# Chunk 0 of a fused attention and MLP kernel: score units on two bank pairs, another order of loads, and idle TensorE time filled for longer

## The chip, the cores and the metric

One core of a Trainium2 chip. The metric is device time in microseconds (us) of one execution. Three runs of the kernel before took 676.94, 677.34 and 677.88 us; their median is 677.34.

## The reference

Attention with 4 sink keys and a window of 128, then an MLP whose activation is a leaky ReLU with a slope per hidden unit. All inputs are fp32; q, k and v are 4 x 8 x 768 x 64 (batch, heads, sequence, head size), the MLP is 512 to 2048 to 512 on 3072 tokens.

```python
scores = scale * np.matmul(q, k.transpose(0, 1, 3, 2))
keep = is_sink | in_window          # pos_k < 4, or 0 <= pos_q - pos_k < 128
scores = np.where(keep, scores, -1000000000.0)
scores = scores - np.max(scores, axis=-1, keepdims=True)
a = np.exp(scores)
a = a / (np.sum(a, axis=-1, keepdims=True) + 1e-09)
...
x = np.ascontiguousarray(attn_out.transpose(0, 2, 1, 3)).reshape(B * S, H * D)
h = x @ w_in
g = np.maximum(h, 0.0) + alpha * np.minimum(h, 0.0)
return (g @ w_out).astype(np.float32)
```

## The kernel before, in words

**Chunks.** The 3072 tokens are 12 chunks of 256 (three per batch entry). For each chunk the attention of 8 heads gives x, transposed, in a high and a low part (xh, xl); then come 16 blocks f of 128 hidden units. gemm1(c, f) makes h from three products per slice of x (high x high, low x high, high x low: L894), ACT and DVE make g and split it into gh and gl (L898 to L901), and gemm2(c, f) adds g times the second weight block to two PSUM banks (L929 to L932). Weights arrive as float64, 1 MB per block, and are split into a high and a low fp32r part on the chip: ACT takes the magnitude (L382), DVE shifts and merges bits (L386, L387, L396; for f from 8 on L394), then the high part is cast (L401; ACT by default, DVE where the planner finds that earlier) and DVE subtracts for the low part (L404). gemm1(c, f) waits for the whole split block f.

**Attention of chunks 0 and 1 (SPLIT).** Two heads share a tile with their q and k in rows 0 to 63 and 64 to 127, `pairs` in DRAM. A score unit is (pair of heads, half u of the queries): two matmuls of 64 rows each into two PSUM banks (L588), then per head DVE's masked minimum (L610, which reads the bank) and ACT's exp (L614). For u = 0 of chunk 0 a unit has 132 columns instead of 260, since there are no earlier keys. After both halves PE transposes the softmax (L633, L634), ACT or DVE copies it out (`comb`, L638, L639), POOL copies the sink columns (L625); after four heads follow the sink tiles `ts` (L689, L690, transposed at L708, read out at L711 as `sinkT`), the reciprocal sums (`ob`, L679, L820), the products with v (L786), and xh and xl (L837, L841, L845). gemm1(0, 0) reads the first xl.

**PSUM.** Eight banks in four kinds of two: `s` for scores (banks 0, 1), `pa` for transposes and products (2, 3), `h` for gemm1 (4, 5), `o` for gemm2 (6, 7; chunk 0's attention borrows them for transposes). In the rows of the instruction order below the banks are numbered from 64, so `s` is 64 and 65, `pa` 66 and 67, `h` 68 and 69, `o` 70 and 71. pt_87 to pt_89 are the three softmax tiles, wa_95 and wa_96 the two work tiles of the weight split, w_305 the first split weight block.

**What sets the order.** All work is written down as operations with a cost, and a planner (`draw`) simulates the five engines, picking by time and rank and giving out tiles as they come free; `issue` then emits the instructions in that order, so each engine runs a fixed queue, in order. Chunk 0's attention goes first; `work` spreads the later chunks' attention over the gemm steps: chunk 1's over OVER = 4 of the first LEAD = 7 steps. Loads of the start are issued by SP in the order in which the program lists them: parameters, three head pairs, weight block 0, the rows `vs` for the sinks, the fourth pair, v, weight blocks 1 to 3, chunk 1's pairs.

**Fillers.** While the plan's time is below WARM = 28 us, `issue` fills a gap before a PE operation with idle matmuls (L1086, 128x512, bf16), each counted as 0.22 us (0.44 in the first 5 us). They all write bank 5, the second `h` bank. 35 of them are in the program.

Of the kernel before, what the change touches and what calls it, by code (L numbers as in the profile page):

```python
# [19 lines left out]
P = 128  # L20
B, H, S, D = 4, 8, 768, 64
DM, DF = 512, 2048
NS = 4
WIN = 2 * P + NS
QC = 2 * P
KC = 3 * P + 2 * NS
# [7 lines left out]
WAIT = {"DVE": 0.2, "ACT": 0.2, "PE": 0.1}  # L34
FILL = 0.22
COLD = 5.0
WARM = 28.0
PENALTY = 0.3
LATEST = 12
BIG = 1e30  # L40
# [2 lines left out]
SPLIT = (0, 1)  # L43
PAIRED = 3
LEAD = 7
OVER = 4
LATE = 14
SPAN = 12
AHEAD = 4
# [29 lines left out]
class Plan:  # L79
# [6 lines left out]
    def __init__(self, tc):  # L86
        self.tc, self.nc = tc, tc.nc
        self.free, self.turn = {}, {}
        self.ops, self.rank, self.last = [], 0, {}

    def kind(self, name, tiles):
        self.free[name] = [(0.0, t) for t in tiles]
# [60 lines left out]
    def draw(self, start, shift=None, until=None):  # L153
# [17 lines left out]
        clock = dict.fromkeys(self.ENGINES, start)  # L171
# [3 lines left out]
        while len(steps) < len(ops):  # L175
# [43 lines left out]
            o, e, t = best[3:]  # L219
            for x in o.ways:  # L220
                open_[x].remove(o)
            got = []
            for v in o.takes:
                if v not in at:
# [34 lines left out]
    def issue(self, steps, fill=None, until=0.0):  # L259
        for o, e, t, clock, got in steps:  # L260
            for v, tile_ in got:
                v.at = tile_
            if e == "PE" and fill and t < until:
                step = FILL * (2 if t < COLD else 1)
                while t - clock > step + 0.2:
                    self.emit(fill)
                    clock += step
            self.emit(o.ways[e][1])

# [52 lines left out]
def program(ctx, tc, qk, pairs, vp, vq, vs, w, par, out):  # L322
# [109 lines left out]
    def bound(v):  # L432
        if v.at is None:
            v.at = v.bind()
        return v.at

    def load_head(c, h):
        if c in SPLIT and h % 2:
            stage[c, h] = stage[c, h - 1]
            return  # L440
        t = stage[c, h] = val("stage") if c else early[h // 2]
        src = pairs[c, h // 2] if c in SPLIT else qk[c, h]
        op("SP", ISSUE, lambda: nc.sync.dma_start(bound(t), src), writes=[t], nbytes=4 * P * (QC + KC))

    def load_v(c, p):
        if c == 0:
            two = early_v[p:p + 2]
            vtile[c, p], vtile[c, p + 1] = two

            def run():  # L450
                for t in two:
                    bound(t)
                nc.sync.dma_start(two[0].box["tile"][:, p:p + 2].rearrange("p n a h d -> p n (a h d)"),
                                  vp[c, p:p + 2].rearrange("n p x -> p n x"))
            op("SP", ISSUE, run, writes=two, nbytes=8 * P * 6 * D)
            return
        t = vtile[c, p] = val("v")
        op("SP", ISSUE, lambda: nc.sync.dma_start(t.at.rearrange("p a h d -> p (a h d)"), (vq if c >= PAIRED else vp)[c, p]),
           writes=[t], nbytes=4 * P * 6 * D)
# [21 lines left out]
    def then(run):  # L481
        n = len(plan.ops)
        run()
        for o in plan.ops[n:]:
            if o.nbytes or o is plan.ops[n]:
                o.rank = len(plan.ops) - 1000
    then(lambda: setup("SP", ISSUE, lambda: nc.sync.dma_start(param, par), (), ("param",)))
    then(lambda: load_head(0, 0))
    then(lambda: load_head(0, 2))
    then(lambda: load_head(0, 4))  # L490
    then(lambda: load_weights(0, "SP"))
    then(lambda: vs_prep(0))
    then(lambda: load_head(0, 6))
    then(lambda: load_v(0, 0))
    then(lambda: load_v(0, 2))
    for f in range(1, FIRST):
        then(lambda: load_weights(f, "SP"))
# [54 lines left out]
    def prep_head(c, h):  # L552
        st = stage.pop((c, h))
        if c in SPLIT:
            r = slice(h % 2 * D, (h % 2 + 1) * D)
            prep[c, h] = (st, r)
            return
        kq = val("kq")
        ks, qh, ql = [lambda s=s: kq.at[:, s] for s in (slice(0, KC), slice(KC, KC + QC), slice(KC + QC, KC + 2 * QC))]
        q_raw, k_raw = lambda: st.at[:, :QC], lambda: st.at[:, QC:]  # L560
        op("ACT", cast(KC), lambda: nc.scalar.copy(ks(), k_raw()), reads=[st], writes=[(kq, "k")])  # L561
        op("ACT", cast(QC), lambda: nc.scalar.copy(qh(), q_raw()), reads=[st], writes=[(kq, "q")])
        op("DVE", dve(KC), lambda: nc.vector.tensor_tensor(ks()[D:], k_raw()[D:], ks()[D:].bitcast(F32), ALU.subtract),  # L563
           reads=[st], writes=[(kq, "k")])
        op("DVE", dve(QC), lambda: nc.vector.tensor_tensor(ql(), q_raw(), qh().bitcast(F32), ALU.subtract),
           reads=[st, (kq, "q")], writes=[(kq, "l")])
        prep[c, h] = (kq, qh, ql, ks)

    def unit(c, h, u):
        if h == 0 and u == 0:  # L570
            nms[c], sink[c], sums[c] = val("nm"), val("sink"), val("sm")
            if c in SPLIT:
                s0 = sink[c]
                op("POOL", 0.15, lambda: nc.gpsimd.memset(s0.at, 0.0), writes=[s0])
        ko = u * (P + NS)
        qs = slice(u * P, (u + 1) * P)
        w0 = slice(0 if c % CPB or u else P, WIN)
        n = w0.stop - w0.start
        kw = slice(ko + w0.start, ko + WIN)
        if c in SPLIT:  # L580
            pair = (h, h + 1)
            banks_ = [val("s") for _ in pair]
            used = [prep[c, h][0]]

            def scores():
                for x, bk in zip(pair, banks_):
                    st, r = prep[c, x]
                    nc.tensor.matmul(bk.at[:, w0], st.at[r, :QC][:, qs], st.at[r, QC:][:, kw], start=True, stop=True)  # L588
            op("PE", 1.47 * native(n), scores, reads=used, writes=banks_, tail=N_TAIL, mode="row")
        else:  # L590
            pair = (h,)
            banks_ = [val("s")]
            kq, qh, ql, ks = prep[c, h]

            def scores():
                s = banks_[0].at
                nc.tensor.matmul(s[:, w0], qh()[:, qs], ks()[:, kw], start=True, stop=False)  # L597
                nc.tensor.matmul(s[:, w0], ql()[:, qs], ks()[:, kw], start=False, stop=True)  # L598
            op("PE", 2 * mm(n), scores, reads=[kq], writes=banks_, tail=R_TAIL)
        for x, bk in zip(pair, banks_):  # L600
            soften(c, x, u, bk)
# [480 lines left out]
    idle = const.tile([P, 2], BF16, name="idle")  # L1082
    plan.emit(lambda: nc.vector.memset(idle, 0.0))

    def fill():
        nc.tensor.matmul(banks[5], idle[:, :1].broadcast_to([P, P]), idle[:, 1:].broadcast_to([P, 512]), start=True, stop=True)  # L1086
    plan.link()
    span, steps = plan.draw(0.8)
    plan.issue(steps, fill, WARM)
# [69 lines left out]
def general(nc, gen, ptile, cc, b, qk5, vp5, nsink, window, ident):  # L1159
# [20 lines left out]
    for h in range(H):  # L1180
        q = gen.tile([D, QC], F32, tag="q", name="q")
        k = gen.tile([D, S], F32, tag="k", name="k")
        v = gen.tile([P, S // P, D], F32, tag="v", name="v")
        nc.sync.dma_start(q, qk5[b, cc, h, 0:D, 0:QC])
        for n in range(CPB):
            nc.sync.dma_start(
                k[:, n * QC:(n + 1) * QC].rearrange("p (a x) -> p a x", a=2),
                qk5[b, n, h, 0:D, QC + P:].rearrange("p (a x) -> p a x", a=2)[:, :, NS:])
            nc.sync.dma_start(v[:, 2 * n:2 * n + 2], vp5[b, n, h // 2, :, 1:3, h % 2])
        po = (h % 2) * D  # L1190
        for u in range(2):
# [86 lines left out]
```

## Time and profile before

| | us |
|---|---|
| median of three runs | 677.34 |
| span of the profiled execution | 676.2 |
| PE busy | 663.8 |
| DVE busy | 525.8 |
| ACT busy | 397.5 |
| POOL busy | 34.5 |

The profiled execution is known by its span, from its first to its last instruction; 1.1 us lie between that and the median of the runs, outside the span. PE's busy time includes fillers, and matmuls overlap with their own weight loads (PEld), so a matmul's listed length is longer than the distance to the next one. In timeline rows the columns are start, length, engine, line, operation, tiles, shapes, and in brackets the idle time before it with what ended it. Rows of a table by stretches are explained where they stand.

### The profile page before, as it was taken

Reading aid. Unit: us, or ns where it says so; the run is one execution under the profiler, and the core shown is the slowest. Engines: PE = TensorE matmul, PEld = TensorE weight load, DVE = VectorE, ACT = ScalarE, POOL = GpSimd, SP = SyncE. Lnnn points to the kernel's source line nnn. Section 1 sums busy time; section 2 is a strip of 40 time slices with the busy share of each in tenths; the row PEclk is TensorE's granted clock in tenths of the full one; section 3 lists DMA queues with packets and bytes.
Section 4 is the critical chain, followed back from the end, with each engine's and each line's share of the span. In section 5 each row is a group of like instructions: output and inputs, shape, how many; then the busy total and the mean of one; then the engine's idle time right before and its main releaser. Section 6 shows DMA issues by size and latency. Waiting matters only on the chain.

```text
span 676.2 us, 13243 instructions
## 1 busy us (share of the span) xinstructions
PE 663.8 (98%) x4532; PEld 580.5 (86%) x4534; DVE 525.8 (78%) x1750; ACT 397.5 (59%) x1066; POOL 34.5 (5%) x115
## 2 busy tenths in 40 slices
PE   9989999999999999999999999999999999999996
PEld 4577898888989989989988988988998988998995
DVE  6999999968967976986986995995895994994331
ACT  6989888827636726736636735644744753853332
POOL 2110000001000000000000000010000000000000
PEclk9979999999999999999999999999999999999999
DMA  8684641424343453443443433552542543420001
GB/s 314 229 277 151 241 187 39 127 71 147 122 133 107 122 148 93 145 132 95 141 118 114 143 107 93 163 140 61 172 128 78 161 128 88 142 94 17 32 2 35
DMA packets 58683, 85.19 MB, mean 126 GB/s; under 512 B 9072, under 2 KB 35056, under 8 KB 58608
## 3 DMA queue, kind: packets, MB, share of 16 engines
q1 hardware_dynamic: 55056, 71.17, 34.7%
q10 hardware_dynamic: 3552, 13.11, 5.4%
q8 instruction: 37, 0.61, 0.4%
q14 instruction: 38, 0.31, 0.1%
HBM read 67.22 MB, written 17.04 MB: 125 GB/s over the span
## 4 chain that ended last, share of the span: by engine, by line
PE 83%; DVE 9%; ACT 5%; issue 2%; POOL 0%; DMA 0%; ACTq 0%; SPq 0%; POOLq 0%
PE bank L894 35%; PE bank L931 12%; PE bank L932 11%; PE bank L929 11%; PE bank L786 3%; PE bank L598 3%; PE bank L597 3%; PE bank L875 2%; DVE wa L396 2%; ACT pt L614 1%; ACT wa L382 1%; DVE wa L394 1%; DVE w L404 1%; DVE g L899 1%; DVE gl L901 1%
## 5 line engine op out<-in xcount | busy, mean ns | idle before, releaser
L894 PE MATMUL bank<-xh,w 128*128 128x256 f32 x1536 | 307.9, 283 | 0.4 <-DVE g L899 0.2
L894 PEld LDWEIGHTS bank<-xh,w 128*128 128x128 f32 x1536 | 250.6, 189 | 9.0 <-DVE g L899 3.0
L894 PE MATMUL bank<-xl,w 128*128 128x256 f32 x768 | 215.1, 280 | 0.1
L898 ACT ACTIVATE g<-bank,param 128x256 f32<-128x256 f32 x192 | 90.5, 472 | 117.4 <-PE bank L894 113.1
L931 PE MATMUL bank<-w,gh 128*128 128x512 f32 x382 | 151.7, 397 | 0.2 <-ACT gh L900 0.2
L932 PE MATMUL bank<-w,gh 128*128 128x512 f32 x382 | 150.1, 393 | 0.0
L894 PEld LDWEIGHTS bank<-xl,w 128*128 128x128 f32 x768 | 145.2, 189 | 4.4 <-DVE xl L808 0.3
L614 ACT ACTIVATE pt<-pt,nm 128x260 f32<-128x260 f32 (+1 forms) x192 | 94.5, 493 | 53.5 <-DVE nm L610 53.1
L899 DVE TENSOR_TENSOR g<-bank,g 128x256 f32<-128x256 f32 x192 | 79.7, 419 | 51.4 <-ACT g L898 50.9
L929 PE MATMUL bank<-w,gl 128*128 128x512 f32 x382 | 119.5, 394 | 0.0
L900 ACT CAST gh<-g 128x256 fp32r<-128x256 f32 x192 | 76.9, 404 | 59.7 <-DVE g L899 59.6
L901 DVE TENSOR_TENSOR gl<-g,gh 128x256 fp32r<-128x256 f32 x192 | 80.5, 423 | 26.5 <-ACT gh L900 23.0
L610 DVE CUSTOM_DVE_ANT_0 pt<-bank,masks 128x260 f32<-128x260 f32 (+1 forms) x192 | 75.0, 401 | 19.3 <-PE bank L598 15.5
L929 PEld LDWEIGHTS bank<-w,gl 128*128 128x128 f32 x382 | 70.7, 188 | 16.2 <-issue 0.7
L931 PEld LDWEIGHTS bank<-w,gh 128*128 128x128 f32 x382 | 71.9, 188 | 9.5 <-ACT gh L900 0.7
L932 PEld LDWEIGHTS bank<-w,gh 128*128 128x128 f32 x382 | 71.9, 188 | 8.3
L563 DVE TENSOR_TENSOR kq<-stage,kq 64x392 fp32r<-64x392 f32 x80 | 45.3, 566 | 2.7
L659 POOL TENSOR_TENSOR sink<-pt,ri 128x8 f32<-128x8 f32 x80 | 20.8, 264 | 504.7 <-DVE ri L644 358.8
L597 PE MATMUL bank<-kq 128*128 128x260 f32 (+1 forms) x160 | 44.4, 278 | 1.3 <-DVE nm L610 1.3
L598 PE MATMUL bank<-kq 128*128 128x260 f32 (+1 forms) x160 | 45.0, 281 | 0.0
L655 DVE CUSTOM_DVE_ANT_0 comb<-pt,ri 128x128 f32<-128x128 f32 x136 | 43.1, 343 | 0.4
L561 ACT CAST kq<-stage 128x392 fp32r<-128x392 f32 x80 | 40.9, 512 | 0.7 <-ACT pt L614 0.2
(130 smaller groups left out, 686.9 us busy)
## 6 DMA issues: line engine op xcount, KB each, us to landing
stage<-qk SPq DMA_DIRECT2D x80, 324.0 KB, 2.9
wraw<-w ACTq DMA_DIRECT2D x12, 1024.0 KB, 5.9
swap<-comb SPq DMA_DIRECT2D x36, 256.0 KB, 2.0
comb<-swap SPq DMA_DIRECT2D x36, 256.0 KB, 3.2
v<-vq SPq DMA_DIRECT2D x36, 192.0 KB, 2.5
out_dram<-ob SPq DMA_DIRECT2D x22, 256.0 KB, 3.5
wraw<-w SPq DMA_DIRECT2D x4, 1024.0 KB, 12.0
v<-vp SPq DMA_DIRECT2D x8, 192.0 KB, 6.9
```

The source lines that it names most:

```text
L597: nc.tensor.matmul(s[:, w0], qh()[:, qs], ks()[:, kw], start=True, stop=False)
L598: nc.tensor.matmul(s[:, w0], ql()[:, qs], ks()[:, kw], start=False, stop=True)
L610: op("DVE", dve(n), lambda: nc.vector.tensor_tensor_reduce(out=pt.at[:, u, w0], in0=s.at[:, w0], in1=masks[:, i, w0], scale=-0.125, scalar ...
L614: op("ACT", exp(n), lambda: nc.scalar.activation(pt.at[:, u, w0], pt.at[:, u, w0], AF.Exp, bias=nm.at[:, h, u:u + 1], scale=-1.0, accum_ou ...
L894: nc.tensor.matmul(h(), fin.at[:, 0, part, ks], rhs.at[:, kt], start=(kt == 0 and n == 0), stop=(kt == KT - 1 and n == 2))
L898: op("ACT", act(QC, True), lambda: nc.scalar.activation(g.at, h(), AF.Copy, scale=alt[:, f:f + 1]), reads=[bk, known("param")], writes=[g])
L899: op("DVE", dve(QC), lambda: nc.vector.tensor_tensor(g.at, h(), g.at, ALU.max), reads=[bk], writes=[g])
L900: op("ACT", cast(QC), lambda: nc.scalar.copy(gh.at, g.at), reads=[g], writes=[gh])
L901: op("DVE", dve(QC), lambda: nc.vector.tensor_tensor(gl.at, g.at, gh.at.bitcast(F32), ALU.subtract), reads=[g, gh], writes=[gl])
L929: nc.tensor.matmul(o2[j].at, gl.at[:, js], fin.at[:, 1, 0], start=False, stop=(f == NF - 1))
L931: nc.tensor.matmul(o2[j].at, gh.at[:, js], fin.at[:, 1, 0], start=(f == 0), stop=False)
L932: nc.tensor.matmul(o2[j].at, gh.at[:, js], fin.at[:, 1, 1], start=False, stop=False)
```

## The change

Five things, all at the start of the program:

- Chunk 0's score units take the bank pairs `s` and `h` in turn: u = 0 in `s`, u = 1 in `h` (gemm1 does not use `h` yet).
- SP's order: weight block 0 comes right behind the first head pair, ahead of the other pairs; the first v load comes ahead of the fourth pair.
- q is stored behind k in the tile, so that chunk 0's loads can leave out the 128 keys that it never reads (128x520 instead of 128x648), and the first third of v.
- Fillers are allowed up to WARM = 44 us of the plan, and each goes to a bank that the plan calls vacant at that time, the first found among the kinds `h`, `s`, `pa`, `o`; where there is none, nothing is filled.
- OVER = 5: chunk 1's attention is spread over five steps instead of four.

In the changed kernel the lines after these edits are numbered 2 or 3 higher (L610 is L613, L404 is L406, L1086 is L1089).

```diff
-WARM = 28.0
+WARM = 44.0
-OVER = 4
+OVER = 5
@@ draw
+            if e == "PE":
+                self.vacant[o] = next((f[0][1] for f in map(free.get, ("h", "s", "pa", "o")) if f and f[0][0] <= clock[e]), None)
@@ issue
-            if e == "PE" and fill and t < until:
+            if e == "PE" and fill and t < until and self.vacant[o] is not None:
                 step = FILL * (2 if t < COLD else 1)
                 while t - clock > step + 0.2:
-                    self.emit(fill)
+                    self.emit(lambda: fill(self.vacant[o]))
@@ load_head
+        seen = slice(0 if c else P, KC + QC)
-        op("SP", ISSUE, lambda: nc.sync.dma_start(bound(t), src), writes=[t], nbytes=4 * P * (QC + KC))
+        op("SP", ISSUE, lambda: nc.sync.dma_start(bound(t)[:, seen], src[:, seen]), writes=[t], nbytes=4 * P * (seen.stop - seen.start))
@@ load_v, chunk 0
-                nc.sync.dma_start(two[0].box["tile"][:, p:p + 2].rearrange("p n a h d -> p n (a h d)"),
-                                  vp[c, p:p + 2].rearrange("n p x -> p n x"))
+                nc.sync.dma_start(two[0].box["tile"][:, p:p + 2, 1:].rearrange("p n a h d -> p n (a h d)"),
+                                  vp[c, p:p + 2, :, 2 * D:].rearrange("n p x -> p n x"))
@@ the first loads
     then(lambda: load_head(0, 0))
+    then(lambda: load_weights(0, "SP"))
     then(lambda: load_head(0, 2))
     then(lambda: load_head(0, 4))
-    then(lambda: load_weights(0, "SP"))
     then(lambda: vs_prep(0))
+    then(lambda: load_v(0, 0))
     then(lambda: load_head(0, 6))
-    then(lambda: load_v(0, 0))
     then(lambda: load_v(0, 2))
@@ unit
-            banks_ = [val("s") for _ in pair]
+            banks_ = [val("h" if c == 0 and (h // 2 * 2 + u) % 2 else "s") for _ in pair]
@@ fill
-    def fill():
-        nc.tensor.matmul(banks[5], idle[:, :1].broadcast_to([P, P]), idle[:, 1:].broadcast_to([P, 512]), start=True, stop=True)
+    def fill(bank_):
+        nc.tensor.matmul(bank_, idle[:, :1].broadcast_to([P, P]), idle[:, 1:].broadcast_to([P, 512]), start=True, stop=True)
```

Every `draw` runs again with these numbers, so the order moves on all engines. Two places matter for what follows. The first is DVE's queue in chunk 0, from the second half of the first head pair on; before it stood so (ISA is the masked minimum; the rows that read out its result are left out):

```order
L610 ISA pt_87,nm_99<-bank_64,masks 128x260
L610 ISA pt_88,nm_99<-bank_65,masks 128x260
L610 ISA pt_89,nm_99<-bank_64,masks 128x132
L610 ISA pt_87,nm_99<-bank_65,masks 128x132
L639 COPY comb_91<-bank_70 128x384
L610 ISA pt_89,nm_99<-bank_64,masks 128x260
L610 ISA pt_87,nm_99<-bank_65,masks 128x260
L386 TENSOR_SCALAR wa_95<-wa_95 128x1024
L467 TENSOR_TENSOR vs_112<-ob_113,vs_112 64x512
L674 TENSOR_SCALAR ri_103<-sm_101 128x8
L689 CAST ts_110<-sink_97 128x4x32
```

The same place in the changed kernel:

```order
L613 ISA pt_87,nm_99<-bank_68,masks 128x260
L613 ISA pt_88,nm_99<-bank_69,masks 128x260
L642 COPY comb_91<-bank_70 128x384
L388 TENSOR_SCALAR wa_95<-wa_95 128x1024
L613 ISA pt_89,nm_99<-bank_64,masks 128x132
L613 ISA pt_87,nm_99<-bank_65,masks 128x132
L613 ISA pt_89,nm_99<-bank_68,masks 128x260
L613 ISA pt_87,nm_99<-bank_69,masks 128x260
L389 SCALAR_TENSOR_TENSOR wa_95<-wraw,wa_95 128x1024
L613 ISA pt_88,nm_99<-bank_64,masks 128x132
L677 TENSOR_SCALAR ri_103<-sm_101 128x8
L692 CAST ts_110<-sink_97 128x4x32
```

The comb copy and the first weight step have moved ahead of the second pair's units, the second weight step has moved ahead of the sink tiles, and the `vs` row behind them.

The second place is PE's queue in chunk 1, where the profile shows PE idle before the third pair's units (stage_79 and stage_80 are the tiles of chunk 1's head pairs). Before:

```order
L588 MATMUL bank_64<-stage_80 128x260
L588 MATMUL bank_65<-stage_80 128x260
L633 MATMUL bank_66<-ident,pt_88 128x128
L634 MATMUL bank_66<-ident,pt_88 128x128
L633 MATMUL bank_67<-ident,pt_89 128x128
L634 MATMUL bank_67<-ident,pt_89 128x128
L588 MATMUL bank_64<-stage_79 128x260
L588 MATMUL bank_65<-stage_79 128x260
```

The same place in the changed kernel (the idle matmul stands there four times, each with its weight load):

```order
L591 MATMUL bank_64<-stage_80 128x260
L591 MATMUL bank_65<-stage_80 128x260
L636 MATMUL bank_67<-ident,pt_88 128x128
L637 MATMUL bank_67<-ident,pt_88 128x128
L1089 LDWEIGHTS idle
L1089 MATMUL bank_70<-idle 128x512
L636 MATMUL bank_66<-ident,pt_89 128x128
L637 MATMUL bank_66<-ident,pt_89 128x128
L934 MATMUL bank_70<-w_305,gh_121 128x512
L935 MATMUL bank_70<-w_305,gh_121 128x512
L591 MATMUL bank_64<-stage_79 128x260
L591 MATMUL bank_65<-stage_79 128x260
```

Four fillers and the first half of gemm2(0, 0) have moved in between two score units; that half stood behind chunk 1's first products before. In all there are 30 fillers now, none after these four.

More of the change, by code (lines that the diff above doesn't have):

```diff
@@ L88, in __init__ @@
         self.free, self.turn = {}, {}
-        self.ops, self.rank, self.last = [], 0, {}
+        self.ops, self.rank, self.last, self.vacant = [], 0, {}, {}
     def kind(self, name, tiles):
@@ L452, in run @@
                     bound(t)
-                nc.sync.dma_start(two[0].box["tile"][:, p:p + 2].rearrange("p n a h d -> p n (a h d)"),
-                                  vp[c, p:p + 2].rearrange("n p x -> p n x"))
-            op("SP", ISSUE, run, writes=two, nbytes=8 * P * 6 * D)
+                nc.sync.dma_start(two[0].box["tile"][:, p:p + 2, 1:].rearrange("p n a h d -> p n (a h d)"),
+                                  vp[c, p:p + 2, :, 2 * D:].rearrange("n p x -> p n x"))
+            op("SP", ISSUE, run, writes=two, nbytes=8 * P * 4 * D)
             return
@@ L559, in prep_head @@
         ks, qh, ql = [lambda s=s: kq.at[:, s] for s in (slice(0, KC), slice(KC, KC + QC), slice(KC + QC, KC + 2 * QC))]
-        q_raw, k_raw = lambda: st.at[:, :QC], lambda: st.at[:, QC:]
+        q_raw, k_raw = lambda: st.at[:, KC:], lambda: st.at[:, :KC]
         op("ACT", cast(KC), lambda: nc.scalar.copy(ks(), k_raw()), reads=[st], writes=[(kq, "k")])
@@ L587, in scores @@
                     st, r = prep[c, x]
-                    nc.tensor.matmul(bk.at[:, w0], st.at[r, :QC][:, qs], st.at[r, QC:][:, kw], start=True, stop=True)
+                    nc.tensor.matmul(bk.at[:, w0], st.at[r, KC:][:, qs], st.at[r, kw], start=True, stop=True)
             op("PE", 1.47 * native(n), scores, reads=used, writes=banks_, tail=N_TAIL, mode="row")
@@ L1183, in general @@
         v = gen.tile([P, S // P, D], F32, tag="v", name="v")
-        nc.sync.dma_start(q, qk5[b, cc, h, 0:D, 0:QC])
+        nc.sync.dma_start(q, qk5[b, cc, h, 0:D, KC:])
         for n in range(CPB):
@@ L1187, in general @@
                 k[:, n * QC:(n + 1) * QC].rearrange("p (a x) -> p a x", a=2),
-                qk5[b, n, h, 0:D, QC + P:].rearrange("p (a x) -> p a x", a=2)[:, :, NS:])
+                qk5[b, n, h, 0:D, P:KC].rearrange("p (a x) -> p a x", a=2)[:, :, NS:])
             nc.sync.dma_start(v[:, 2 * n:2 * n + 2], vp5[b, n, h // 2, :, 1:3, h % 2])
@@ L1238 @@
         for half in (slice(0, D), slice(D, P)):
-            qk[:, c, :, half, :QC] = qT[:, c]
-            o = QC
+            qk[:, c, :, half, KC:] = qT[:, c]
+            o = 0
             for n, i in enumerate(blocks):
```

## Prediction

> **What bounds the kernel now.** I read four views: the page, a table by stretches, the chain that ended last in order of time, and the timeline of the first 75 us. First the page's busy times, and the table by stretches (start:end, length, then the busy us of PE, PEld, DVE, ACT and POOL with their instructions, the granted clock, DMA share, GB/s).
>
> ```profile
> PE 663.8 (98%) x4532; PEld 580.5 (86%) x4534; DVE 525.8 (78%) x1750; ACT 397.5 (59%) x1066; POOL 34.5 (5%) x115
> ```
>
> ```profile
> 6.00:14.00 8.00, 7.63 (x44) 3.79 (x43) 4.74 (x21) 6.34 (x21) 1.00 (x4) 1.00 1.00 381
> 14.00:34.00 20.00, 19.10 (x130) 11.88 (x131) 19.37 (x50) 19.12 (x51) 2.91 (x6) 1.00 0.71 257
> 34.00:44.00 10.00, 8.27 (x38) 6.41 (x39) 9.38 (x26) 9.01 (x25) 2.33 (x4) 0.66 0.85 310
> 44.00:70.00 26.00, 25.16 (x181) 20.28 (x182) 24.85 (x42) 21.94 (x47) 0.86 (x2) 1.00 0.57 188
> 70.00:97.00 27.00, 26.97 (x177) 24.35 (x176) 26.63 (x42) 23.55 (x40) 0.00 (x0) 1.00 0.55 200
> 115.00:670.00 555.00, 553.48 (x3839) 495.84 (x3839) 420.15 (x1515) 299.83 (x850) 23.62 (x82) 1.00 0.37 109
> ```
>
> PE's 98% is an average over stages that differ. From 115 to 670 us PE is busy 553.5 of 555 us with matmuls of the reference, and the change leaves those matmuls alone; little is to be won there. Before 44 us PE's busy time holds idle filling and waiting. From 14 us on DVE is the full engine: 19.37 of 20 us, then 9.38 of 10, 24.85 of 26, 26.63 of 27. It has slack only from 6 to 14 us (8 - 4.74 = 3.26 us), from 34 to 44 (0.62) and from 44 to 70 (1.15). So the start is a race of DVE through softmax, weight splitting and the first g tiles, and PE fills up behind it. From 70 us both are full, and there DVE is just in time:
>
> ```profile
> 68.89 1.22 DVE L404 TENSOR_TENSOR w<-wa,w 128x1024 fp32r<-128x1024 f32 x1
> 69.98 0.28 PE L894 MATMUL bank<-xh,w 128*128 128x256 f32 x1
> 74.82 0.19 PEld L894 LDWEIGHTS bank<-xh,w 128*128 128x128 f32 x1 [0.46 <-DVE g L899]
> ```
>
> The eighth weight block is finished by DVE at 70.1 us and its first matmul begins at 70.0, nothing between; at 74.82 PE waits for DVE again. What DVE gains before 70 us therefore comes off the end one for one, provided PE is not behind it. Next the chain in order of time (start, us, what), cut to where PE stands on it:
>
> ```profile
> 5.08 1.60 PE bank L1086 x5
> 6.68 0.64 PE bank L588 x4
> 7.69 1.09 PE bank L1086 x5
> ...
> 38.36 1.58 PE bank L588 x4
> 40.56 2.56 PE bank L894 x12
> ```
>
> Two things are to be seen. Early, the chain runs through idle matmuls (L1086): they stand ahead of a score unit that could not start anyway, because its two banks were still being read. Later it runs through PE at half clock (0.66 on average from 34 to 44 us).
>
> **The change, part by part.**
>
> *Two bank pairs and the second unit at once (chunk 0).* DVE's waits in that stretch:
>
> ```profile
> 7.35 0.43 DVE L610 CUSTOM_DVE_ANT_0 pt<-bank,masks 128x260 f32<-128x260 f32 x1 [1.04 <-PE bank L588]
> 9.23 0.30 DVE L610 CUSTOM_DVE_ANT_0 pt<-bank,masks 128x132 f32<-128x132 f32 x1 [1.10 <-PE bank L588]
> 10.89 0.43 DVE L610 CUSTOM_DVE_ANT_0 pt<-bank,masks 128x260 f32<-128x260 f32 x1 [0.51 <-PE bank L588]
> 12.01 0.69 DVE L386 TENSOR_SCALAR wa<-wa 128x1024 int32<-128x1024 int32 x1 [0.34 <-ACT wa L382]
> 18.33 1.23 DVE L404 TENSOR_TENSOR w<-wa,w 128x1024 fp32r<-128x1024 f32 x1 [0.42 <-ACT w L401]
> 22.26 0.69 DVE L845 TENSOR_TENSOR xl<-ob,xh 128x512 fp32r<-128x512 f32 x1
> ```
>
> They sum to 1.04 + 1.10 + 0.51 + 0.34 + 0.42 = 3.41 us ahead of xl, which opens the first gemm1. With four banks the first pair's four L610 run back to back: the last ended at 7.35 + 2 x 0.43 = 8.2, and without the first wait it ends at 7.1. What is late next is on ACT (and POOL, last row):
>
> ```profile
> 8.33 0.50 ACT L614 ACTIVATE pt<-pt,nm 128x260 f32<-128x260 f32 x1
> 9.61 0.48 ACT L638 COPY comb<-bank 128x384 f32<-128x384 f32 x1 [0.68 <-PE bank L634]
> 10.77 1.12 ACT L382 ACTIVATE wa<-wraw 128x1024 f32<-128x1024 f32 x1
> ...
> 13.05 0.69 POOL L625 COPY sink<-pt 128x8 f32<-128x8 f32 x2 [3.88 <-ACT pt L614]
> ```
>
> The pair's last exp starts at about 7.4 instead of 8.33, so the transposes behind it and DVE's comb copy come at about 8.7 instead of 9.6. In the new order DVE takes that copy and the first weight step ahead of the second pair, and so waits twice: from 7.1 to 8.7 (1.6 us) for the copy, 0.5 long; and from 9.2 to 9.9 (0.7) for ACT, which behind its last exp (8.1) has its own comb copy (0.48) and the first weight step (1.12 and a short read of its sum). The second pair's four L610 then run without a wait. A third wait is new: the sink tiles (L689) now come before the vs row, and follow POOL's two copies (0.69) behind the second pair's exps, another 0.7. The 0.42 before L404 goes: the first block's high part moves from ACT (L401) to DVE, for which the trace has no row; the nearest are L386 (0.69) and L404 (1.23), same 128x1024, and I take 0.69, being a one-input row. Against it one comb copy moves from DVE to ACT, about half a us either way. Sum on DVE: 1.6 + 0.7 + 0.7 = 3.0 for 3.41, and 0.1 because one bad row moves behind the first L610: **0.5 us earlier**, between 0 (each removed wait returns) and 1.0 (the first pair's lead survives).
>
> In the rows of DVE's queue that stand with the change, the copy and the weight step have moved ahead of the second pair: this is where two of the removed waits return.
>
> *First weight block second, unread keys not loaded.* What the loads bring in the first stretches (last column GB/s):
>
> ```profile
> 2.00:4.00 2.00, 2.00 (x6) 0.45 (x3) 1.21 (x9) 0.10 (x1) 0.79 (x5) 1.00 0.86 237
> 4.00:6.00 2.00, 1.91 (x8) 0.91 (x8) 1.90 (x13) 0.00 (x0) 0.54 (x2) 1.00 1.05 286
> 6.00:8.00 2.00, 2.00 (x13) 0.91 (x11) 0.96 (x7) 1.06 (x5) 0.00 (x0) 1.00 0.85 327
> ```
>
> The block now ends 0.01 (parameters) + 0.27 (one shortened pair tile) + 1.05 MB into the queue, 1.33 MB; 237 and 286 GB/s bring 1.05 MB by 6 us and 327 the rest by 6.9. ACT needs it at about 8.7. That cover is 1.8 us; beyond it the price is 1 for 1. The three pair tiles, the vs rows and the v tiles that it passes on SP come later or as before: the second pair tile, behind the block, at about 1.59 MB or 7.7 us, and its scores are not due before 9. SP does nothing here but issue loads. The 0.5 MB not loaded are hidden: apart from the first pair tile no wait on a DMA stands on this stretch of the chain. I put nothing on this part.
>
> *Fill until 44 us.* The half clock and what precedes it (PE rows, then one short stretch):
>
> ```profile
> 31.97 0.39 PE L894 MATMUL bank<-xh,w 128*128 128x256 f32 x2
> 35.69 1.08 PE L588 MATMUL bank<-stage 64*128 64x260 f32 x4 [1.19 <-DVE nm L610]
> 40.78 0.63 PE L894 MATMUL bank<-xh,w 128*128 128x256 f32 x2
> ```
>
> ```profile
> 30.00:32.00 2.00, 1.69 (x12) 1.04 (x12) 2.00 (x5) 1.97 (x6) 0.80 (x2) 1.00 0.79 177
> ```
>
> An idle of 0.31 us in 2 left the clock at 1.00; one of 1.19 was followed by the halving. The Trainium skill (TensorE: Matmul & The Clock Gate, "Why this matters for your kernels") asks only that PE-idle gaps stay under about 3 us. By that rule the 1.19 us gap would have been harmless, the fillers worth nothing, and the sum 676.2 - 0.5 + 1.1 = 676.8; the trace, with the clock at 0.66 behind that gap, disagrees. In the new order, as the rows of PE's queue show, four fillers and the first half of gemm2 of the first weight block stand in that gap. At full clock the chain's pieces shrink: L894 by the ratio 0.63 to 0.39 (2.56 to 1.6), L588 from 1.58 to 0.64: 0.96 + 0.94, PE is some 1.9 us earlier at 44 us. DVE caps what this is worth, since it was itself full. What it can regain is what it lost behind a late PE, from the waits between 43 and 56 us (us in all, times, longest):
>
> ```profile
> ACT comb L638 <- PE bank L634: 1.2, 1, 1.2
> DVE w L404 <- ACT w L401: 0.9, 2, 0.5
> ...
> DVE ts L689 <- POOL sink L625: 0.2, 1, 0.2
> DVE pt L610 <- PE bank L588: 0.2, 1, 0.2
> ```
>
> ACT stood 1.2 us for a transpose, and DVE then for ACT. The DVE waits make 0.9 + 0.2 + 0.2 = 1.3 us, all its idle from 34 to 70 us 0.62 + 1.15 = 1.77. I take **1.2**, between 0 and 1.77.
>
> *Chunk 1 over five slots instead of four.* The same instructions, weight steps earlier, the second half of chunk 1's xl one weight row (1.22, as L404) later on DVE. Before it PE now has half a gemm2 more in hand; cost between 0 and 1.2, I take 0.
>
> *Sum.* 676.2 - 0.5 - 1.2 = 674.5 us of span. The runs' median, 677.34, lies 1.1 above the span (start and end outside it): 674.5 + 1.1 = **675.6 us**. About 0.2% (1.35 us) is what a measurement of this kernel can tell from no change.
>
> **The rivals.**
>
> *A: the clock falls all the same, only later.* Filling ends at 44 us of the plan. A PE that is 1.9 us earlier waits for DVE in every slot up to 70 us, unfilled; gaps near 1 us lie between the 0.31 that was harmless and the 1.19 that was not. Two slow windows there bring the DVE waits (1.3) back. For it: DVE's 24.85 of 26. Against: PE has gemm2 work in hand. Or the later xl of chunk 1 eats the gain. Time 677.3 - 0.5 = 676.8, with either only in part 676.2: no change that can be told. The 1.19 us row is why I keep it.
>
> *B: the weight block comes late and holds both queues.* New in the order: ACT's first weight step and DVE's stand ahead of the second pair's softmax, so a late block stops both. The four blocks loaded by SP took (KB each, median us from issue to landing):
>
> ```profile
> wraw<-w SPq DMA_DIRECT2D x4, 1024.0 KB, 12.0
> ```
>
> Issued third, at about 1.7 us, it would land by that median at 13.7, 5.0 after the need: 675.6 + 5.0 = 680.6. It decides from 8.7 us on, and the kernel is slower by over 0.2% from 8.7 + 1.7 + 1.35 = 11.8. Against it: those 12 us are of blocks behind one to four megabytes of other loads, and the bytes give 6.9.
>
> *C: PE is held by its own fillers.* They now write any bank that the plan calls vacant; where its reader is late, filler and all behind it wait on PE, up to 44 us. DVE's fullness hides that too, unless it opens idle that halves the clock again close to 70 us, where PE's busy 26.97 of 27 leaves nothing to catch up with. A slow stretch lasts 6.8 us here (half of 10 us at 0.66 is 3.4 us lost), so 3.4 us on top of 675.6: 679.0.
>
> **How the numbers follow.** Forecast 0.53 (its range 674.5 to 676.2), A 0.33, B 0.07, C 0.07. The forecast gives faster, save its upper edge, which A's partial form makes up for; A gives no change; B and C give slower. Faster 0.53, same 0.34, slower 0.13. The range reaches from the forecast with both terms near their upper ends (676.2 - 1.0 - 1.77 = 673.4, drawn in to 674.4 since both at once are unlikely) to A's upper end with a little of chunk 1's cost: 677.5.
>
> **What would show it.** Right: the first pair's four L610 (L613 in the changed kernel) without a wait, DVE waiting once before the comb copy; xl about 0.5 us earlier than 22.26; clock 1.00 from 34 to 44 us; L404 (now L406) waiting for ACT less than its 0.9 in all between 43 and 56; the eighth block's split ending near 68.4. Wrong: clock under 1.00 between 44 and 70 us (A), ACT's first weight step waiting for a DMA (B), a PE wait before a filler or the clock down after 70 us (C). If the eighth block is 1.7 us earlier and the end is not, then DVE is not what sets the start of the full stretch.

## The result, and the profile after

The changed kernel takes 673.34 us (five executions, 673.06 to 674.51) where before takes 677.34: 4.0 us less, ratio 0.9941 with a 95% interval of 0.9929 to 0.9952. That is 2.3 us below the forecast of 675.6 and 1.1 below the low end of the range. The span of its profiled execution is 671.4 us instead of 676.2. One kernel of those below, `no_sign`, also had two slow executions (809 and 1667 us), which its row leaves out.

The table by stretches of the changed kernel (columns as before: busy us of PE, PEld, DVE, ACT, POOL, then granted clock, DMA share, GB/s):

```profile
6.00:14.00 8.00, 7.11 (x38) 3.73 (x38) 5.88 (x25) 6.93 (x23) 1.41 (x4) 1.00 1.04 396
14.00:34.00 20.00, 18.84 (x132) 12.16 (x132) 19.78 (x51) 19.31 (x53) 3.13 (x6) 1.00 0.69 243
34.00:44.00 10.00, 9.90 (x77) 7.50 (x76) 9.81 (x24) 9.57 (x25) 2.47 (x4) 1.00 0.83 300
44.00:70.00 26.00, 23.91 (x164) 19.45 (x164) 25.73 (x47) 24.54 (x50) 0.96 (x2) 1.00 0.65 231
70.00:97.00 27.00, 26.46 (x170) 23.67 (x170) 26.84 (x41) 23.96 (x41) 0.00 (x0) 1.00 0.52 182
115.00:670.00 555.00, 550.07 (x3819) 493.11 (x3817) 415.88 (x1493) 298.32 (x843) 23.57 (x81) 1.00 0.37 110
```

DVE's idle time before 70 us has halved: 2.12, 0.22, 0.19 and 0.27 us in the first four rows where it was 3.26, 0.63, 0.62 and 1.15. The clock of the third row is 1.00 where it was 0.66. The last row answers to before's 553.48 of 555 us: PE reaches 115 us with more of its work behind it, so it is the end of the program that moves into that stretch.

DVE's waits in chunk 0, and the two rows that the prediction spoke of further on (timeline of the changed kernel):

```profile
8.34 0.56 DVE L642 COPY comb<-bank 128x384 f32<-128x384 f32 x1 [1.46 <-PE bank L637]
9.48 0.69 DVE L388 TENSOR_SCALAR wa<-wa 128x1024 int32<-128x1024 int32 x1 [0.58 <-ACT wa L384]
...
11.22 1.22 DVE L389 SCALAR_TENSOR_TENSOR wa<-wraw,wa 128x1024 int32<-128x1024 int32 x1
...
12.76 0.23 DVE L692 CAST ts<-sink 128x128 fp32r<-128x128 f32 x1
...
20.43 0.69 DVE L848 TENSOR_TENSOR xl<-ob,xh 128x512 fp32r<-128x512 f32 x1
...
65.23 1.22 DVE L406 TENSOR_TENSOR w<-wa,w 128x1024 fp32r<-128x1024 f32 x1
```

```profile
66.26 0.28 PE L897 MATMUL bank<-xh,w 128*128 128x256 f32 x1
```

Two waits stand where five stood, 1.46 + 0.58 = 2.04 us instead of 3.41. The xl that opens the first gemm1 starts at 20.43 instead of 22.26 us, the eighth weight block is split at 66.4 instead of 70.1, and its first matmul follows at once, as before. That fits DVE as the bound up to there, still, only 3.7 us earlier.

### The profile page after: what moved, and what is told of

Its sections match the earlier page's. It is cut to its first block, busy times and chain, and to the rows that moved or that the text cites. A ratio compares the mean times of both kernels' runs of the same rounds, so it can differ in the third digit from the quotient of the medians.

```text
span 671.4 us, 13234 instructions
## 1 busy us (share of the span) xinstructions
PE 658.9 (98%) x4529; PEld 577.5 (86%) x4529; DVE 524.7 (78%) x1750; ACT 397.2 (59%) x1066; POOL 34.5 (5%) x115
## 4 chain that ended last, share of the span: by engine, by line
PE 83%; DVE 11%; ACT 2%; issue 1%; POOL 0%; DMA 0%; ACTq 0%; DVEq 0%
PE bank L897 36%; PE bank L934 12%; PE bank L932 12%; PE bank L935 12%; PE bank L789 3%; PE bank L600 3%; PE bank L601 3%; PE bank L878 2%; DVE wa L398 2%; DVE w L406 2%; DVE wa L396 1%; DVE wa L389 1%; DVE pt L613 1%; ACT pt L617 1%; DVE gl L904 1%
## 5 line engine op out<-in xcount | busy, mean ns | idle before, releaser
L613 DVE CUSTOM_DVE_ANT_0 pt<-bank,masks 128x260 f32<-128x260 f32 (+1 forms) x192 | 75.0, 401 | 14.9 <-PE bank L601 13.7
```

What stands on the lines that cost most here:

```text
L613: op("DVE", dve(n), lambda: nc.vector.tensor_tensor_reduce(out=pt.at[:, u, w0], in0=s.at[:, w0], in1=masks[:, i, w0], scale=-0.125, scalar ...
```

## The experiments

All ratios are to the kernel before on the same chip; its medians there were 677.17 to 677.40 us. The intervals are 0.6 to 1.0 us to each side.

| | median us | ratio, 95% interval |
|---|---|---|
| chunk0_alone | 675.32 | 0.9967 (0.9954 to 0.9980) |
| fill_alone | 676.29 | 0.9982 (0.9973 to 0.9990) |
| five_slots_alone | 675.47 | 0.9966 (0.9954 to 0.9978) |
| no_chunk0 | 675.26 | 0.9971 (0.9961 to 0.9980) |
| no_late_fill | 674.12 | 0.9947 (0.9933 to 0.9962) |
| no_five_slots | 674.37 | 0.9955 (0.9941 to 0.9969) |
| fill_until_62 | 673.35 | 0.9940 (0.9926 to 0.9953) |
| old_loads | 676.07 | 0.9979 (0.9968 to 0.9989) |
| new_loads_alone | 676.95 | 0.9994 (0.9983 to 1.0004) |
| old_block | 675.85 | 0.9977 (0.9968 to 0.9985) |
| banks_alone | 675.38 | 0.9976 (0.9967 to 0.9985) |
| no_sign | 677.16 | 0.9996 (0.9983 to 1.0009) |
| low_twice | 679.63 | 1.0029 (1.0017 to 1.0040) |
| six_slots | 676.37 | 0.9981 (0.9972 to 0.9990) |
| late_13 | 672.98 | 0.9944 (0.9929 to 0.9958) |
| late_15 | 674.72 | 0.9961 (0.9948 to 0.9974) |

### The parts, alone and left out

The change falls into three parts: chunk 0 (bank pairs and loads), the fill until 44 us, and the five slots. Six kernels have one or two of the three; with before and the changed kernel that makes all eight combinations. Chunk 0's part moves some 20 rows in the queues of PE, DVE and ACT, all before 21 us; the fill moves none; the five slots move 160 to 190 rows of PE and DVE, up to about 160 us.

`chunk0_alone` is the changed kernel with

```diff
-WARM = 44.0
+WARM = 28.0
-OVER = 5
+OVER = 4
```

> Of the changed kernel only the chunk 0 part: two bank pairs, first weight block second, unread keys not loaded; fillers end at 28 us of the plan and chunk 1 is spread over four slots, as before. Behind chunk 0 the order of the instructions is that of before. The first theory here (chunk 0 gives what the changed kernel's first gemm1 shows, 22.9 to 21.0 us, because two of the three waits put on record do not come): 1.9 us less than before, 675.4, and the half clock from 36 us on stays. The step on record: 0.5 us less, 676.8. The rival (what chunk 0 gains is lost again in the slow stretch from 34 to 44 us): xl earlier by 1.9 us and the time within 0.4 us of before.

2.0 us less, and xl at 20.21 us. The first theory holds: chunk 0's gain is four times the step on record, and it reaches the end whole. It is not lost in the slow stretch, which is still there (a clock of 0.66 from 34 to 44 us).

`fill_alone` is before with the vacant banks and WARM = 44:

> The kernel before with fillers up to 44 us of the plan, each in a vacant bank; every other instruction in the order of before (47 fillers instead of 35). The step on record: clock 1.00 from 34 to 44 us and 1.2 us less, 676.1 (bounds 677.3 and 675.6). The rival on record (the clock falls later): 677.3, with a stretch under 1.00 between 44 and 70 us. A second rival: the clock gives more than 1.2, up to the 4.0 us of the whole change, 673.3.

1.0 us less. The clock stays at 1.00; this table's row of the stretch answers to before's 0.66:

```profile
34.00:44.00 10.00, 9.92 (x72) 6.74 (x74) 9.73 (x26) 9.23 (x26) 2.03 (x4) 1.00 0.80 302
```

`five_slots_alone` is before with OVER = 5:

> The kernel before with chunk 1's attention over five slots instead of four (its order of instructions is that of the changed kernel up to some 20 rows of each engine), all else as before, fillers up to 28 us. The step on record: no gain, 677.3 (at worst 1.2 more, 678.5). The rival that puts the missing gain here (weight blocks are split earlier, PE has more in hand): 1 to 2 us less, 675.3 to 676.3.

1.8 us less: the rival's number comes, and the step on record falls. The rival's reason, weight blocks split earlier, is tested further on. Alone the three parts give 2.0 + 1.0 + 1.8 = 4.8, together 4.0. The next three kernels show where 0.8 is shared.

`no_late_fill` is the changed kernel with WARM = 28:

> The changed kernel with fillers up to 28 us of the plan only (26 instead of 30; every other instruction stands where it stood). If the fill is worth what was put on record: 1.2 us more than the changed kernel, 674.5, with a stretch at half clock between 30 and 50 us. If it is worth nothing in the new order, since half a gemm2 stands in the gap already: 673.3 and the clock stays at 1.00. If all of the gain hangs on the clock: 676 or more.

By the median 0.8 us more, but the executions fall into two groups: 673.13, 673.35 and 673.39, as the changed kernel, and 674.84, 674.86 and 675.05. Up to 52 us its gemm1 steps start within 0.1 us of the changed kernel's and the clock is 1.00; the profiled one, of the second group, loses its clock only at 57.5 us. PE's wait is there again, 1.04 us where the fillers stood:

```profile
33.50 0.33 PE L636 MATMUL bank<-ident,pt 128*128 128x128 f32 x1 [1.04 <-ACT comb L641]
```

But the half gemm2 that five slots moved follows right behind it. So in the new order the clock holds between 34 and 44 us without the four late fillers, in this execution, as it does in that of `five_slots_alone` (1.00). That is a gain which fill and five slots share.

`no_five_slots` is the changed kernel with OVER = 4, `no_chunk0` the one with the bank pairs and loads undone:

> The changed kernel with chunk 1 over four slots again (chunk 0's part and the fill until 44 us stay). From the parts alone (chunk 0 2.0 us, fill 1.0): 677.2 - 3.0 = 674.2 if they add up. If the fill is worth as little here as in the changed kernel: 675.2. No exec with the half clock between 34 and 44 us is expected either way.

> The changed kernel with chunk 0 as before (one bank pair, the loads as before); fill until 44 us and five slots stay. If chunk 0's 2.0 us are independent of the rest: 673.3 + 2.0 = 675.3, with the first gemm1 at 22.4 us and the time behind it as in the changed kernel. If the three parts share one gain (DVE catches up anyway): 674 or less.

674.37 and 675.26. Chunk 0 and fill add up (3.0 us less). Fill and five slots do not: together they give 2.1 where the two alone make 2.8, so most of the missing 0.8 is theirs. Beside the fill, chunk 0 is worth 1.9 us and five slots 1.0. Taken in that order, the 4.0 us are 2.0 chunk 0, 1.0 clock, 1.0 five slots.

### The clock

`fill_until_62` is the changed kernel with WARM = 62:

> The changed kernel with fillers up to 62 us of the plan (37 instead of 30, seven of them between the fifth and the seventh weight block; nothing else moves). The theory of the window (the clock is halved for the 3.4 us that follow a window of 3.4 us in which PE works less than about 0.4 of the time; the grid of windows starts elsewhere in every execution, and the changed kernel has one such stretch, near 55 us, that some executions catch): no execution at half clock between 44 and 70 us, all executions near 673.2, none over 674. The rule of the 1.2 us gap (the clock falls behind a long gap wherever it lies): as the changed kernel, since its gaps there are under 0.9 us, 673.3 with the same spread. Rival: the fillers hold PE up, 673.6 to 674.5.

673.18 to 673.64 in five executions, none higher, while the changed kernel had one of five at 674.51 and `no_late_fill` three of six near 675; five executions are few to call that shown. The median does not move. What precedes a halving can be read where the table is cut at the 3.41 us steps that the clock keeps in each execution. First before, then `five_slots_alone`, then the changed kernel (the window ahead, and what follows):

```profile
33.18:36.59 3.41, 2.22 (x13) 1.31 (x12) 3.38 (x8) 3.03 (x8) 0.26 (x1) 1.00 0.98 328
36.59:40.00 3.41, 2.87 (x10) 1.70 (x10) 3.25 (x11) 3.02 (x8) 0.71 (x2) 0.50 1.04 420
```

```profile
55.12:58.53 3.41, 1.91 (x11) 1.00 (x10) 3.38 (x5) 3.41 (x7) 0.00 (x0) 1.00 0.53 173
58.53:61.94 3.41, 3.41 (x20) 2.65 (x22) 3.15 (x6) 2.80 (x7) 0.00 (x0) 0.50 0.73 207
```

```profile
55.08:58.49 3.41, 2.27 (x19) 1.51 (x19) 3.41 (x6) 3.40 (x7) 0.00 (x0) 1.00 0.82 311
58.49:61.91 3.42, 3.42 (x36) 2.98 (x33) 3.42 (x6) 2.88 (x8) 0.00 (x0) 1.00 0.87 285
```

A thin window (13 or 11 matmuls) is followed by a whole window at 0.50; one with 19 is not, though two of its matmuls start as far apart, 0.95 us, as in the second. But neither the count nor the gap decides. Behind a window of `banks_alone` with 10 matmuls, two of whose gaps are longer (1.23 and 1.06 us from start to start), the clock stays full. So it does in `new_loads_alone`, which has before's order: its window holds nearly the same matmuls as the first one above, with the same idle in it (1.17 us; 1.19 in before). First `banks_alone`, then `new_loads_alone`:

```profile
51.40:54.80 3.40, 1.81 (x10) 1.00 (x8) 3.30 (x8) 3.25 (x9) 0.00 (x0) 1.00 0.00 0
54.80:58.20 3.40, 3.25 (x28) 2.51 (x30) 3.40 (x5) 3.29 (x8) 0.00 (x0) 1.00 0.79 279
```

```profile
32.99:36.40 3.41, 2.25 (x14) 1.31 (x12) 3.38 (x8) 3.03 (x7) 0.23 (x1) 1.00 0.84 296
36.40:39.82 3.42, 2.38 (x14) 1.57 (x14) 3.26 (x11) 3.04 (x8) 0.73 (x2) 1.00 1.03 417
```

So a thin window can cost the clock and need not. What the clock counts, and where the limit lies, these runs do not show. The Trainium skill (TensorE: Matmul & The Clock Gate, "What's actually happening") says that a window of 3413 ns, free-running and not reset by the kernel, decides the clock; the half stretches here, 3.41 and 6.83 us long and on another grid in every profiled execution, agree with it. In the same section the Trainium skill has the clock halved after an idle window; here a window was enough in which PE was listed as busy for 1.91 to 2.22 of 3.41 us.

An execution without a trace is known by its mean clock alone. That counts the last 0.5 to 3.7 us too, which are at half clock in every profile: the 0.997 of `fill_alone`'s profiled execution is that alone.

### Chunk 0: banks, block or bytes

`old_loads` keeps every queue of the changed kernel but SP's:

```diff
+    sp = [i for i, s in enumerate(steps) if s[1] == "SP"][:9]
+    old = [steps[sp[i]] for i in (0, 1, 3, 4, 2, 5, 7, 6, 8)]
+    for i, s in zip(sp, old):
+        steps[i] = s
...
-        op("SP", ISSUE, lambda: nc.sync.dma_start(bound(t)[:, seen], src[:, seen]), writes=[t], nbytes=4 * P * (seen.stop - seen.start))
+        op("SP", ISSUE, lambda: nc.sync.dma_start(bound(t), src), writes=[t], nbytes=4 * P * (seen.stop - seen.start))
```

> The changed kernel with the loads as they were: SP issues the first weight block behind three head pairs again, the fourth pair ahead of v, and whole tiles are loaded (128x648, all three thirds of v). Every other instruction stands where it stands in the changed kernel. If the two bank pairs alone give chunk 0's 2.0 us and the loads nothing (the step on record): 673.3, as the changed kernel. The rival (the block now comes just in time, and the new order of the queues needs it): ACT's first weight step and all behind it wait for the block, 0.5 to 2 us more, 674 to 675.3.

2.7 us more than the changed kernel, beyond the rival's range. ACT in its timeline, then DVE:

```profile
7.84 0.48 ACT L641 COPY comb<-bank 128x384 f32<-128x384 f32 x1
10.55 1.12 ACT L384 ACTIVATE wa<-wraw 128x1024 f32<-128x1024 f32 x1 [2.23 <-DMA wraw<-w]
```

```profile
11.80 0.69 DVE L388 TENSOR_SCALAR wa<-wa 128x1024 int32<-128x1024 int32 x1 [2.90 <-ACT wa L384]
```

The block arrives at 10.5 us. In before ACT reads it at 10.77, without a wait; in the new order ACT wants it at 8.3, with DVE's first weight step and the second pair's four L613 queued behind.

`old_block` undoes only SP's order and keeps the shortened loads. `new_loads_alone` is before with the new loads, its queues kept. `banks_alone` is before with the bank pairs, planned afresh:

> The changed kernel with only the order of SP's first loads undone (block behind three pairs, fourth pair ahead of v); the unread keys and the first third of v stay left out, and all other instructions keep their order. If the block's place is what chunk 0 needs: ACT's first weight step waits for its DMA about as in the run with all old loads (2.2 us), less the 0.25 MB of unread keys ahead of it at some 300 GB/s (0.7 us), so 1.5 us more than the changed kernel, 674.8. If it is the bytes: 673.4.

> The kernel before with the new loads only: first weight block second, v ahead of the fourth pair, unread keys and the first third of v left out; all else in the order of before. If the loads give nothing by themselves: 677.3. The rival (half of chunk 0's gain is the loads'): 676.3.

> The kernel before with the two bank pairs only (old loads, fill until 28 us, four slots); the planner draws a new order, which differs from that of before and of the changed kernel by some 200 rows on PE and DVE. If the bank pairs give the gain by themselves where the planner knows the loads: 675.2. If they need the block second: 676.7 to 677.4, with DVE or ACT waiting for the block or for scores before 15 us.

`old_block` loses 2.5 us where 1.5 were expected, with this wait:

```profile
9.76 1.12 ACT L384 ACTIVATE wa<-wraw 128x1024 f32<-128x1024 f32 x1 [1.44 <-DMA wraw<-w]
```

The wait itself is as estimated (1.44). More than the wait is lost: PE, idle for 1.61 us up to 12 us, is at half clock from 13.8 to 17.2. `new_loads_alone` gives nothing that can be told. `banks_alone` gives 1.8 us with the old loads, but only in part in chunk 0: its gemm1(0, 0) starts at 22.07 us, 0.8 earlier than in before, where `chunk0_alone` has 20.83, 2.05 earlier. Its order is another one up to about 160 us, and at gemm1(1, 9) it is 1.1 us behind before (119.9 and 118.8). So the bank pairs with the old loads are worth 0.8 us at the first gemm1; that they alone give chunk 0's 2.0 is not shown. The block's place gives nothing by itself, but is the condition of the order that the planner drew with it, in which ACT and DVE take the block ahead of the second pair. The bytes matter where the block is late: the wait is 1.44 us with the shortened loads and 2.23 without, the profiled spans 673.5 and 674.0, the medians 0.2 apart.

### Five slots

I took the gain at first for DVE's lead: the last weight block is split at 105.2 us in the changed kernel, at 114.4 in before. Two kernels change DVE's work there. `no_sign` is before without the sign step for f from 13 on; `low_twice` is the changed kernel with this:

```diff
+        def low_part():
+            for again in range(2 if f >= 12 else 1):
+                nc.vector.tensor_tensor(fin.at[:, :, 1], wf(), fin.at[:, :, 0].bitcast(F32), ALU.subtract)
```

> The kernel before without the sign step (L398, 1.14 us of DVE each) of the last three weight blocks: those blocks lose the signs of their weights. DVE is relieved of 3.4 us between 93 and 113 us; all else stands in the order of before. The theory (spreading chunk 1 over five slots gains because DVE finishes the weight blocks sooner, so that chunk 2's score units no longer wait for its masked minimum, 0.43, 0.38 and 0.26 us at 112 and 126 us, and more near 152 to 156): 1.0 to 1.9 us less, 675.4 to 676.2, and those waits of PE gone. The rival (five slots gain by what they do ahead of 100 us): 677.3, since nothing there changes.

> The changed kernel with the subtraction for the low part (L406) of the last four weight blocks done twice, the same result each time: DVE has 4.9 us more to do between 86 and 110 us, and the last block is finished near 110 instead of 105.2. The theory (DVE being ahead at 110 us is worth what five slots gained): most of 1.85 us comes back, 674.4 to 675.2, with PE waits for the masked minimum between 110 and 130 us. The rival: DVE's lead there is spare, 673.3.

`no_sign` gives no gain. Its mean clock went down to 0.992, lower than that of most executions of before, so I compare its profiled span, which had no half clock before its end, with that of `fill_alone`, which had none either and the same order: 673.9 and 674.7. In this pair 3.4 us less of DVE work are worth 0.8. Of PE's three waits for the masked minimum between 70 and 160 us in before (1.3 us in all) two remain (1.0). The theory falls. `low_twice` costs 6.3 us by the median, and 5.0 between the profiled spans (676.4 and 671.4), which had no half clock before their end: all of the added 4.9. PE waits for DVE's masked minimum there (waits of PE from 97 to 130 us; the line numbers are 2 higher in this kernel):

```profile
PE bank L602 <- DVE nm L615: 4.6, 2, 3.4
```

So DVE has no lead to spare in the changed kernel up to 111 us either. More work costs in full there; less work, in before's order, gives little.

Where five slots gain is read from `no_five_slots` and the changed kernel, neither with a half clock before its end. Both end the eighth block's split at 66.4 us. At the sixteenth block's gemm1(0, 15) five slots are still 0.4 us behind (112.6 and 112.1), at gemm1(1, 9) 0.7 (115.9 and 115.2). At gemm1(2, 0) the two are level (140.8 and 140.9), and at gemm1(2, 2) five slots are 1.0 us ahead (153.4 and 154.4). `five_slots_alone` and before show the same: level at gemm1(1, 9) (118.9 and 118.8), with the clock lost for 3.41 us in the one and 6.83 in the other by then, and 1.8 ahead at gemm1(2, 2) (156.3 and 158.1). So five slots gain 1.7 to 1.9 us between 115 and 158 us; at full clock they had paid 0.7 ahead of that. Part of the gain stands in the last xl of chunk 2, 1.1 us earlier. DVE in `no_five_slots`:

```profile
65.21 1.22 DVE L406 TENSOR_TENSOR w<-wa,w 128x1024 fp32r<-128x1024 f32 x1
...
148.36 0.43 DVE L613 CUSTOM_DVE_ANT_0 pt<-bank,masks 128x260 f32<-128x260 f32 x1 [2.26 <-PE bank L601]
...
151.81 0.43 DVE L811 TENSOR_TENSOR xl<-bank,xh 128x256 fp32r<-128x256 f32 x1 [0.53 <-ACT xh L808]
```

and in the changed kernel:

```profile
150.52 0.29 DVE L613 CUSTOM_DVE_ANT_0 pt<-bank,masks 128x132 f32<-128x132 f32 x1 [0.41 <-PE bank L601]
...
150.74 0.42 DVE L811 TENSOR_TENSOR xl<-bank,xh 128x256 fp32r<-128x256 f32 x1
```

With four slots a score unit of chunk 3 stands on PE behind gemm2 and twelve products, DVE idles 2.26 us for it, and PE then waits for the xl halves behind it. `no_sign` has the same DVE wait, 2.27 us. That speaks for where the instructions stand, and not for how much DVE has to do. Three kernels move that order without moving what comes before it, or go a slot further:

> The changed kernel with chunk 1 over six slots. If what five slots gained comes from the weight blocks being finished sooner, six go on in that direction: less than 673.3 by up to 1 us. If it comes from where chunk 2's instructions happen to fall in the queues at 110 to 160 us, the new order is another draw: the first gemm1 up to 110 us within 0.7 us of the changed kernel's, and the rest within 2 us either way, 672.5 to 675.5.

> The changed kernel with chunk 2's attention spread over 13 slots instead of 14: nothing moves up to about 95 us, and the queues differ from there to about 160 us. If the five slots' gain lies in where chunk 2's and 3's instructions fall in the queues: a change of 0.5 to 2 us either way, with the first gemm1 equal to the changed kernel's up to 95 us. If DVE's lead sets it: within 0.3 us of 673.3.

> The changed kernel with chunk 2's attention spread over 15 slots: nothing moves up to about 95 us, and the queues differ only from there to about 120 us. If the order at 120 to 160 us sets the gain, and it is the same here: within 0.3 us of 673.3. If any move of chunk 2's start matters: 0.5 us or more either way.

`six_slots` loses 3.0 us against five, outside what either theory gave; its first gemm1 steps agree up to 42 us, but gemm1(1, 0) starts at 65.3 instead of 62.6, so it loses ahead of chunk 2, and its profiled execution has a half-clock window from 58.8 us. `late_13` and the changed kernel cannot be told apart (672.98 and 673.34): up to 1.3 us that its chunk 1 gains near 132 us are gone at 156. `late_15` has a median 1.4 us higher, but four of its five executions had a mean clock of 0.997; the one with 0.999 took 673.80. So neither shows a gain of order by itself, and the forecast of 0.5 to 2 us for `late_13` failed. The traces show the place of what five slots gain; that the queue order there is its cause rests on the waits that vanish, and no run has moved that order alone. This stays open.

None of these kernels is faster than the changed one by more than can be told.

## Why the prediction was wrong, point by point

- **What bounds the kernel: right.** "What DVE gains before 70 us therefore comes off the end one for one": `chunk0_alone` has the eighth block 1.6 us earlier and ends 2.0 earlier, and `low_twice` shows the same up to 111 us. What was wrong is the sentence next to it, that from 115 us on "little is to be won there" because PE is busy 553.5 of 555 us. That row is an average over stages too. Of the 1.52 us that PE is idle in it, 1.02 lie in ten (before):

```profile
150.00:160.00 10.00, 8.98 (x67) 6.86 (x66) 6.99 (x26) 8.02 (x24) 1.50 (x2) 1.00 0.51 154
```

  Five slots gain there and in the 35 us ahead of it.
- **Chunk 0, 0.5 us: the step that failed.** All five waits went, and of the three that I put in their place two came, at nearly the size given: 1.46 for 1.6 and 0.58 for 0.7. The third, 0.7 for the sink tiles behind POOL, did not come. The order rows that I quoted had the second weight step (L389, 1.22 us), one L613 and L677 ahead of those tiles. POOL's copies, below, end at 12.73 us, and DVE is through with L677 at 12.75: the tiles came in time with nothing to spare.

```profile
11.65 1.08 POOL L628 COPY sink<-pt 128x8 f32<-128x8 f32 x2 [3.59 <-ACT pt L617]
```

  So 1.37 us of waits went, not 0.4. Another 0.19 is the first L613 (5.61 instead of 5.80), for which I had 0.1, and the rest of the 1.83 at xl, 0.27, is for the most part idle too short to be listed. The bound of 1.0 was too low with it.
- **Loads, 0: right alone, wrong as a price of their place.** They give nothing by themselves. But the cover that I named (landing 6.9, need 8.7) is what the order lives on: without it the kernel loses 2.7 us. A late block was priced one for one, and that holds for the wait (2.23), not for what is lost behind it, where the clock is halved.
- **Fill, 1.2: the mechanism right, the agent partly wrong.** The clock is worth 1.0 us of the median. In the profiled execution it was worth more, by subtraction 4.8 - 2.0 - 1.0 = 1.8 us; that one had lost two windows of 3.41 us. In the changed order the half gemm2 from the five slots stands in the same place, and in `no_late_fill` the clock held there without the four fillers. That an idle of 1.19 us "was followed by the halving" was misread as its cause: in before's own order 1.17 us at the same place were followed by none (`new_loads_alone`), and in `five_slots_alone` no idle over 0.68 us stood ahead of the halving.
- **Five slots, 0: failed.** I had a cost bounded from 0 to 1.2 and no gain allowed. The cost is there, 0.7 us at 115 us. But behind it come 1.7 us of gain, up to 154 us, that nothing in my reading looked at: the edit names chunk 1, but the planner's order moves up to 160 us. What is left is 1.0, and in `five_slots_alone` the clock held from 34 to 44 us without the late fillers.
- **The base.** I put 1.1 us outside the span, from the median of some executions and the span of another. Each later execution has its own time 1.8 to 2.2 us above its own span, 1.96 in the middle. The profiled execution of before thus took about 678.2, with a clock of 0.994; in later runs of before such executions take 678.3 to 679.1 and those with 0.996 some 677.1. The sum missed the span by 3.1 us (1.5 chunk 0, 1.0 five slots, 0.6 clock) and the base gave some 0.85 back, which was luck: 675.6 - 673.34 = 2.26.
- **The range.** Its foot with both terms high, 673.4, is a span: the 1.1 us outside was left off. As a time it is 674.5, so the 674.4 that I gave was not drawn in at all, and that 673.4 is nearly the result is chance; the span measured was 671.4. And I called both terms high together unlikely, though they had one common ground, a full DVE.
- **The rivals.** A may have had its half-clock window, but not in the median: one execution in five of the changed kernel took 674.51 us with a mean clock of 0.997, without a trace. In `no_late_fill` it came in the profiled execution, and by time and mean clock in half of all. B did not come, and `old_loads` shows what it would have been. C did not come: `fill_until_62` adds seven fillers at no cost.

## What to carry to other kernels

When waits are removed from a queue, count the new ones against the order rows instruction by instruction, with the length of each that stands between; a wait that I carried over in my head was half of chunk 0's missing gain. Where a planner writes the order, an edit in one stage is a new order in every later one until the two rejoin, so compare the queues to the point where they are the same again before a part is put at nothing. Cut a long stretch into short ones before it is called full. Take the base of a sum from one execution's own time and span, and ask whether its clock is that of the median.

## What the runs showed of the hardware that was not expected

- The same program has executions 1.4 to 2 us apart: 673.1 to 673.4 and 674.8 to 675.1 (`no_late_fill`), some 677.2 and 678.3 to 679.1 (before). As a rule the slower ones have the lower mean clock (0.996 or 0.997 against 0.998 or 0.999; 0.994 or 0.995 against 0.996). In the profiled ones the clock is at 0.50 for whole windows of 3.41 us behind a stretch with little TensorE work, but nearly the same stretch cost the clock in before and not in `new_loads_alone`.
- One late load, waited for 2.23 us at 8 us, cost 2.7 us at the end; behind it PE was idle for 2.40 us, and the clock was at 0.50 from 14.3 to 17.7 us.
- 4.9 us more DVE work at 86 to 110 us cost 5.0 in the changed order; 3.4 us less in before's order gave 0.8. Whether the order or the sign of the change makes that difference was not tried.
